# Packed attention and a mixture of experts on one core: batch 0 is routed in two groups of chunks, with batch 1's small products at their ends

## The chip, the cores and the metric

The kernel runs on 1 core of one Trainium2 chip. The metric is device time in microseconds (us) of one execution. The kernel before takes 422.11 us, the median of three runs (421.89 to 422.68). A core has five engines with an instruction queue each: PE (TensorE, matrix products), DVE (VectorE), ACT (ScalarE), POOL (GpSimd) and SP (SyncE, which here only issues transfers). Each runs its queue strictly in order and waits on semaphores for the others.

## The reference, cut to what matters

```python
def sm_attn(qq, kk, vv):                       # for 8 batches x 8 heads, S = 576, D = 64
    s = scale * np.matmul(qq, kk.transpose(0, 1, 3, 2))
    s = s - np.max(s, axis=-1, keepdims=True)
    a = np.exp(s)
    a = a / (np.sum(a, axis=-1, keepdims=True) + 1e-09)
    return np.matmul(a, vv)
p_packed = sm_attn(p, k, v)                    # 32 packed rows a head
attn = sm_attn(q, p_packed, p_packed)          # 576 rows a head
x = attn.transpose(0, 2, 1, 3).reshape(B * S, H * D)       # 4608 x 512

xn, en = x / norm(x), expert_emb / norm(expert_emb)
logits = xn @ en.T / tau                       # 8 experts
expert_idx = np.argmax(logits, axis=1)
gate_w = softmax(logits)[arange(N), expert_idx]
for e in range(8):
    mask = expert_idx == e
    h = np.maximum(x[mask] @ w1[e], 0.0)       # 512 -> 1024
    out[mask] = gate_w[mask, None] * (h @ w2[e])           # 1024 -> 512
```

## The kernel before, in words

The eight batches of 576 rows are worked one after the other. Each batch guesses one expert for all its rows, loads that expert's w1 and w2, and computes the feed-forward network (FFN) with them; rows whose expert turns out to be another one would be done again at the end (none are here). Products are made of 32-bit values split in a high and a low part, in three passes (`PASSES`).

The order of the work is written out by hand: `ffn` of batch b is a generator, and at each of its `yield`s the main loop advances the attention of batch b+1 (`step_att`) and the gates of batch b. For batch 0 the table `PLAN` says, letter by letter, what stands at each yield: `a` a step of batch 1's attention, `d` a transposition of batch 1's queries, `r` a step of batch 0's `route`, `w` one split of a w2 tile, `g` a step of batch 0's gates. Every engine then gets its instructions in the order in which this Python code records them.

The pieces that the change touches, for batches 0 and 1:

- `route` (L752 to L841) makes the attention rows in 5 chunks of 128 (the last of 64) with `product` (L766 on PE), squares them on ACT (L778) and sums the logits on DVE (L781), then finds each row's expert. Each chunk lies in a PSUM tile `pt` of the pool `pb`, which has 2 buffers. Before, batch 0 goes chunk by chunk; all later batches go in two groups, chunks 0 and 1, then chunks 2, 3 and both halves of 4.
- `pack_slowly` (L577) ends batch 1's packed attention: `pair_turn` (L501 on PE), its copy to `T` (L598), `row_logits` (L512 on PE), `logits_out` (L521). Then come `guess` (L619; its product L629, its DVE work L635 to L640, and a register load by SP), the load of w1 (L891), `att2` with `query_scores` (L270 on PE) and the softmax of the second attention, and the load of w2 (L899).
- The softmax works on two halves of the columns, 0 and 1: `unpack` (L675, DVE), `biggest` (L680, DVE), `shift` (L686), `expo` (L689, ACT), `total` (L695 to L697, DVE), `norm` (L701), `turn` (L704, DVE), `high` (L710, ACT), `low` (L715). The string `ENG1` gives for batch 1 the engine of shift 0, shift 1, norm 0, norm 1, low 0 and low 1: `v` is DVE, `p` is POOL.
- `counts` (L846 on PE) counts rows by expert; `gates` (L859 to L881) makes the gate of each row on DVE, with one exponential on ACT (L872); `gates_main` (L1394) adds the sum of the hits.
- In `ffn`, the product L1039 takes the 64 last rows through w2 into a tile `pf`; L1057 takes the four chunks c = 0 to 3 of the others through w2, 24 matmuls each. The tiles `pf` come from the pool `ps`, which has 3 buffers. The L1039 tile is stored (L1406, ACT, scaled by the gate) in the middle of chunk 1; its buffer is the one that chunk 2 of L1057 takes.

```python
    ps = ctx.enter_context(tc.tile_pool(name="ps", bufs=3, space=bass.MemoryType.PSUM))
    ...
                    if f == STF and len(last) > late:
                        store(*last.pop(0))
```

Of the kernel before, what the change touches and what calls it, by code (L numbers as in the profile page):

```python
# [9 lines left out]
F32 = mybir.dt.float32  # L10
# [7 lines left out]
P = 128  # L18
# [9 lines left out]
def kernel(  # L28
# [499 lines left out]
    def att1(x, nat, queries=None, other=None):  # L528

        def pack(queries, other):  # L530
# [46 lines left out]
        def pack_slowly():  # L577
# [16 lines left out]
            yield  # L594
# [10 lines left out]
        if x.halves:  # L605
            for g in range(NG):
                key_max(x, g)
                yield
                key_exp(x, g)
                yield  # L610
            yield from pack_slowly()
        else:
            asked = queries or all_queries(x, nat)
            yield from pack(asked, other)
            if queries is None:
                drain(asked)
# [33 lines left out]
    def att2(x, after=None, first=False, b1=False, eng1="vvvvvv"):  # L650
# [69 lines left out]
        if not first:  # L720
            query_scores(x)
            yield from idle(3 if x is bat[1] else 2)
# [34 lines left out]
    def route(x):  # L757
# [36 lines left out]
        if x is bat[0]:  # L794
            for c in range(NC5):
                pt = units()
                for g in range(NG):
                    product(c, g, pt[:, :, g])
                yield
                sums(c, pt[:, :, :NG], lg[:, c], ss[:, c : c + 1])  # L800
        else:
            lg4 = sm.tile([P, E], F32, name="lg4", tag="lg4", bufs=1)
            ss4 = sm.tile([P, 1], F32, name="ss4", tag="ss4", bufs=1)
            for cs in ((0, 1), (2, 3)):
                pts = [units() for _ in cs]
                for c, pt in zip(cs, pts):
                    for g in range(NG):
                        product(c, g, pt[:, :, g])
                if cs[0]:
                    for g, pt in enumerate(pts):  # L810
                        product(4, g, pt[:, :, NG])
                yield
                for c, pt in zip(cs, pts):
                    sums(c, pt[:, :, :NG], lg[:, c], ss[:, c : c + 1])
                    yield
            sums(4, pts[0][:, :, NG:], lg[:, 4], ss[:, 4:5])
            sums(4, pts[1][:, :, NG:], lg4, ss4)
            yield
            nc.vector.tensor_tensor(out=lg[64:, 4], in0=lg[64:, 4], in1=lg4[64:], op=ALU.add)
            nc.vector.tensor_tensor(out=ss[64:, 4:5], in0=ss[64:, 4:5], in1=ss4[64:], op=ALU.add)  # L820
# [298 lines left out]
    def att_main(b):  # L1119
        x = bat[b]  # L1120
        if b:
# [3 lines left out]
            yield from att1(x, nat_main(b), queries, bat[b - 1] if b > 1 else None)  # L1125
            sync = b == 1
            queue = nc.sync if sync else nc.gpsimd
# [9 lines left out]
        if b:  # L1137
            if b > 1:
                yield
            for _ in range(3 if b == 1 else 2):  # L1140
                yield next(second)
            load_w2(x, x.e, queue)
            if b == 1:
                yield from idle(3)
# [249 lines left out]
    def gates_main(b):  # L1394
        x = bat[b]
        yield from gates(x)
        hit = sm.tile([1, E], F32, name="hit", tag="hit", bufs=1)
# [3 lines left out]
    def store_main(b):  # L1401
# [33 lines left out]
    ENG1 = "vvppvp"  # L1435
# [5 lines left out]
        "aqwd", "aawrr", "awd", "rdwra", "rwa", "rwa", "", "a", "aag", "aag",  # L1441
# [8 lines left out]
    def route_first():  # L1450
        yield from route(bat[0])
        yield from idle(2)
        counts(bat[0])
# [164 lines left out]
```

## Time and profile before

| what | value |
|---|---|
| three runs | 421.89, 422.11, 422.68 us |
| profiled execution | 420.91 us, span 419.2 us from its first to its last instruction |
| mean granted clock of TensorE | 0.995 |
| PE busy | 408.4 us (97% of the span), 4036 matmul records |
| DVE, ACT, POOL busy | 307.2, 202.5, 158.7 us |

The span is what the trace shows; the time of the execution is 1.7 us longer. The profiled execution lies 1.2 us below the median of the three runs, so a difference read from the trace is put onto the median as it is. All start times below are us from the start of the span. In a timeline, instructions of one kind that follow each other are merged into one row: its start, its length to the end of the last one, the count, and in brackets how long the engine was idle before it and what ended that. The records of PE are its passes: a 32-bit matmul has two records, an L1057 matmul one.

### The profile page before, as it was taken

How to read it: one execution, taken by the hardware profiler on the slowest of the kernel's cores; microseconds unless marked ns; L12 is line 12 of the kernel's file. 1: busy time of each engine (PE TensorE's matmuls, PEld its weight loads, DVE VectorE, ACT ScalarE, POOL GpSimd, SP SyncE). 2: the span in 40 equal slices, each digit the busy share in tenths (PEclk: the TensorE clock that was granted, in tenths of full speed). 3: DMA queues.
4: the chain of work that ended last, by engine and by line, in shares of the span. 5: the costliest groups of instructions: out<-in, count | busy, mean ns of one | idle time of the engine just before them, and what ended most of it. 6: DMA issues, size and time to landing. Idle time of an engine off the chain costs nothing.

```text
span 419.2 us, 11033 instructions
## 1 busy us (share of the span) xinstructions
PE 408.4 (97%) x4036; PEld 327.9 (78%) x4037; DVE 307.2 (73%) x941; ACT 202.5 (48%) x473; POOL 158.7 (38%) x197
## 2 busy tenths in 40 slices
PE   7899999999999999999999999999999999999993
PEld 4758677697878978698777978789786987779783
DVE  3677696588977889769886889778897798566500
ACT  4577705762365714754146622656146631576110
POOL 2345714437204561336414381136613273142200
PEclk9999999999999999999999999999999999999998
DMA  8999896977999479886999669886899819310012
GB/s 225 331 338 236 220 296 221 229 189 187 298 298 235 116 216 294 284 201 172 267 316 228 169 172 280 301 216 177 225 317 262 195 39 344 121 48 5 20 48 54
DMA packets 42607, 87.93 MB, mean 210 GB/s; under 512 B 11690, under 2 KB 20906, under 8 KB 42546
## 3 DMA queue, kind: packets, MB, share of 16 engines
q1 hardware_dynamic: 35280, 61.44, 54.2%
q0 software_dynamic: 6720, 25.17, 18.4%
q8 instruction: 34, 0.56, 0.6%
q10 hardware_dynamic: 546, 0.54, 0.6%
q14 instruction: 27, 0.22, 0.2%
HBM read 77.68 MB, written 9.44 MB: 208 GB/s over the span
## 4 chain that ended last, share of the span: by engine, by line
PE 91%; DMA 4%; ACT 1%; DVE 1%; POOL 1%; SPq 0%; issue 0%; ACTq 0%; POOLq 0%
PE pf L1057 43%; PE pf L1004 24%; PE pf L1039 7%; PE pt L766 5%; DMA nat<-in_k 4%; PE pt L934 3%; PE pt L396 2%; PE pt L270 2%; PE pt L331 2%; PE pt L1233 1%; PE pu L501 0%; DMA out<-o 0%; PE pt L477 0%; PE pu L512 0%; ACT st L689 0%; PE pt L464 0%
## 5 line engine op out<-in xcount | busy, mean ns | idle before, releaser
L1057 PE MATMUL pf<-w2s,hT 128*128 128x512 f32 (+1 forms) x792 | 183.9, 388 | 0.0
L1057 PEld LDWEIGHTS pf<-w2s,hT 128*128 128x128 f32 x792 | 143.1, 188 | 39.3 <-issue 9.4
L910 POOL TENSOR_TENSOR w2s<-w2r,w2s 128x512 fp32r<-128x512 f32 x64 | 81.2, 1285 | 86.1 <-ACT w2s L909 85.3
L1004 PE MATMUL pf<-AT,G 128*128 128x288 f32 x720 | 102.1, 298 | 0.4 <-DVE hT L1009 0.2
L1004 PEld LDWEIGHTS pf<-AT,G 128*128 128x128 f32 x720 | 97.2, 188 | 4.3 <-issue 1.5
L1009 DVE SCALAR_TENSOR_TENSOR hT<-pf,hT 128x224 fp32r<-128x224 f32 (+1 forms) x128 | 52.2, 413 | 30.3 <-ACT hT L1008 29.9
L1008 ACT ACTIVATE hT<-pf 128x224 fp32r<-128x224 f32 (+1 forms) x128 | 49.3, 386 | 42.8 <-PE pf L1004 40.1
L1406 ACT ACTIVATE o<-pf,gate 128x512 f32<-128x512 f32 (+1 forms) x41 | 26.0, 635 | 32.2 <-PE pf L1057 21.2
L909 ACT CAST w2s<-w2r 128x512 fp32r<-128x512 f32 x64 | 38.7, 618 | 0.2
L291 DVE STREAM_TRANSPOSE kt<-nat 128x576 f32<-128x576 f32 x52 | 38.1, 759 | 0.0
L778 ACT ACTIVATE scr<-pt 128x512 f32<-128x512 f32 (+2 forms) x47 | 25.0, 532 | 18.0 <-PE pt L766 17.0
L1039 PE MATMUL pf<-w2r,h 128*64 128x256 f32 x256 | 33.3, 388 | 0.0
L715 POOL TENSOR_TENSOR AT<-at,AT 128x576 fp32r<-128x576 f32 x7 | 9.9, 1411 | 49.1 <-ACT AT L710 49.1
L383 POOL TENSOR_TENSOR qs<-p 128x320 f32<-128x320 f32 x12 | 10.6, 881 | 45.4 <-ACT p L364 45.4
L689 ACT ACTIVATE st<-st 128x576 f32<-128x576 f32 (+1 forms) x17 | 11.1, 657 | 33.8 <-DVE st L686 32.6
L872 ACT ACTIVATE lg<-lg 128x40 f32<-128x40 f32 x8 | 1.9, 237 | 48.4 <-DVE lg L868 48.4
L781 DVE TENSOR_REDUCE lg<-pt 128x8 f32<-128x32 f32 (+2 forms) x47 | 8.7, 185 | 22.0 <-ACT scr L778 21.7
L766 PEld LDWEIGHTS pt<-ppx,at 64*128 64x128 f32 x320 | 19.7, 186 | 6.2 <-issue 3.6
L1039 PEld LDWEIGHTS pf<-w2r,h 128*64 128x64 f32 x256 | 19.4, 137 | 4.9 <-PE pu L501 1.0
L766 PE MATMUL pt<-ppx,at 64*128 64x136 f32 x320 | 23.1, 287 | 0.0
L710 ACT CAST AT<-at 128x576 fp32r<-128x576 f32 x15 | 10.1, 675 | 22.6 <-DVE at L704 22.5
L364 ACT ACTIVATE p<-pt,qnm 128x160 f32<-128x160 f32 x48 | 17.8, 398 | 0.0
(213 smaller groups left out, 474.9 us busy)
## 6 DMA issues: line engine op xcount, KB each, us to landing
nat<-in_q SPq DMA_DIRECT2D x112, 140.0 KB, 3.5
nat<-in_k SPq DMA_DIRECT2D x96, 140.0 KB, 4.0
w1t<-in_moe_w POOLq DMA_DIRECT2D x12, 1024.0 KB, 9.3
w2r<-in_moe_w POOLq DMA_DIRECT2D x24, 512.0 KB, 16.0
out<-o SPq DMA_DIRECT2D x124, 64.0 KB, 2.1
w2r<-in_moe_w SPq DMA_DIRECT2D x8, 512.0 KB, 10.3
vn<-in_v SPq DMA_DIRECT2D x24, 160.0 KB, 3.8
vn<-in_v SPq DMA_DIRECT2D x48, 80.0 KB, 3.9
```

The lines of the kernel that those rows point to most:

```text
L291: nc.vector.transpose(kt.rearrange("p (c i) -> p c i", i=32), t)
L364: nc.scalar.activation(x.p1[g][:, n * QW : n * QW + QW], area(x, g)[:, n // 2, n % 2], AF.Exp, bias=x.nm[:, at : at + 1],)
L766: nc.tensor.matmul(to[:, half], x.at[at, g, n : n + P], x.ppx[at, g], start=True, stop=True, tile_position=(64 * half, 0),)
L778: nc.scalar.activation(scr[r, :, : pt.shape[2]], pt[r, :, :, : 2 * D], AF.Square, accum_out=sss[r])
L909: nc.scalar.copy(t[:, 0], raw)
L910: nc.gpsimd.tensor_tensor(out=t[:, 1], in0=raw, in1=t[:, 0].bitcast(F32), op=ALU.subtract)
L1004: nc.tensor.matmul(pf[:, :HS], w, r, start=(n == 0), stop=(n == len(ops) - 1))
L1008: nc.scalar.activation(hT[:, 0, f, cs], pf[:, :n], AF.Relu)
L1009: nc.vector.scalar_tensor_tensor(out=hT[:, 1, f, cs], in0=pf[:, :n], scalar=0.0, in1=hT[:, 0, f, cs].bitcast(F32), op0=ALU.max, op1=ALU.su ...
L1039: nc.tensor.matmul(pf[64 * hf : 64 * hf + 64, :256], h4[:, f], x.w2r[f // 2][:, f % 2, hf * 256 : hf * 256 + 256], start=(f == 0), stop=(f ...
L1057: nc.tensor.matmul(pf[:, :w], hT[:, a, f, c * P : (c + 1) * P], x.w2s[f][:, m, at : at + w], start=(f == 0 and i == 0), stop=(f == NF - 1 ...
L1406: nc.scalar.activation(o[:, :w], pf[:, :w], AF.Copy, scale=x.gate[:, c : c + 1])
```

## The change

Batch 0's `route` now uses the code of the other batches with the groups in the other order: chunks 0, 1 and both halves of 4 in the first group, 2 and 3 in the second. The table `PLAN` puts batch 1's `pair_turn` at the end of the first group and its `row_logits` at the end of the second, and takes several steps of batch 0's FFN between; `query_scores` of batch 1 is recorded before its `guess`, and both stand within the first chunk of L1057. `counts` of batch 0 goes with that of batch 1 into batch 2's attention, and its sum of hits (`hits(0)`) too. Shift 0 of batch 1 goes from DVE to POOL (`ENG1`). The steps of batch 0's gates stand at other places between those of batch 1's softmax.

```diff
             quarter_totals(x, sums)
-            if other:
-                counts(other, pt[:1, 256 : 256 + NC5 * E])
+            for n, other in enumerate(others):
+                counts(other, pt[:1, 256 + n * NC5 * E : 256 + (n + 1) * NC5 * E])
             next(queries)
             yield
-            if other:
+            for other in others:
                 counted(other)
+                if other is bat[0]:
+                    hits(0)
...
-        if not first:
+        if not first and not x.s2:
             query_scores(x)
-            yield from idle(3 if x is bat[1] else 2)
+            yield from idle(2)
...
-        if x is bat[0]:
-            for c in range(NC5):
-                pt = units()
+        lg4 = sm.tile([P, E], F32, name="lg4", tag="lg4", bufs=1)
+        ss4 = sm.tile([P, 1], F32, name="ss4", tag="ss4", bufs=1)
+        for cs in ((0, 1), (2, 3)):
+            pts = [units() for _ in cs]
+            rest = bool(cs[0]) != (x is bat[0])
+            for c, pt in zip(cs, pts):
                 for g in range(NG):
                     product(c, g, pt[:, :, g])
+            if rest:
+                for g, pt in enumerate(pts):
+                    product(4, g, pt[:, :, NG])
+            yield
+            for c, pt in zip(cs, pts):
+                sums(c, pt[:, :, :NG], lg[:, c], ss[:, c : c + 1])
+                if c != 3 or rest:
+                    yield
+            if rest:
+                sums(4, pts[0][:, :, NG:], lg[:, 4], ss[:, 4:5])
+                sums(4, pts[1][:, :, NG:], lg4, ss4)
                 yield
-                sums(c, pt[:, :, :NG], lg[:, c], ss[:, c : c + 1])
...
             sync = b == 1
+            if sync:
+                query_scores(x)
...
-    ENG1 = "vvppvp"
+    ENG1 = "pvppvp"
...
-        "aqwd", "aawrr", "awd", "rdwra", "rwa", "rwa", "", "a", "aag", "aag",
-        "aagr", "agr", "gar", "ga", "gra", "g", "ga", "", "", "a",
+        "awd", "aw", "radw", "ra", "rd", "rw", "w", "w", "ra", "r",
+        "r", "ar", "a", "a", "aa", "ga", "ga", "gga", "gg", "gga",
...
     def route_first():
         yield from route(bat[0])
-        yield from idle(2)
-        counts(bat[0])
```

What this does to three queues is read from the built programs. The first place is PE, from the first L1039 product of batch 0 to its w2 product L1057, whose line is L1053 after the change (L1039 becomes L1035, L766 becomes L767, L629 becomes L630). `ppx,at` are the products of `route`, `ident,ppx` is the pair turn, `enT,T` the row logits, `ppx,itaus` the guess, `kt,T` the query scores, `oh,ones` the counts. Before, the last twelve blocks up to the long one:

```order
L1039 MATMUL pf<-w2r,h_519 64x256 x2
L766 MATMUL pt<-ppx,at 128x136 x8
L1039 MATMUL pf<-w2r,h_519 64x256 x2
L766 MATMUL pt<-ppx,at 128x136 x4
L512 MATMUL pu<-enT,T 64x8 x4
L1039 MATMUL pf<-w2r,h_519 64x256 x2
L629 MATMUL pu<-ppx,itaus 64x8 x2
L1039 MATMUL pf<-w2r,h_519 64x256 x4
L270 MATMUL pt<-kt,T 32x288 x16
L1039 MATMUL pf<-w2r,h_519 64x256 x2
L1057 MATMUL pf<-w2s,hT 128x512 x9
L846 MATMUL pu<-oh,ones 1x40
```

Ahead of these stand four more (L1039 x2, L766 x8, L1039 x2, L501 x2). After the change the whole stretch is:

```order
L1035 MATMUL pf<-w2r,h_519 64x256 x4
L767 MATMUL pt<-ppx,at 128x136 x12
L501 MATMUL pu<-ident,ppx 128x128 x2
L1035 MATMUL pf<-w2r,h_519 64x256 x12
L767 MATMUL pt<-ppx,at 128x136 x8
L512 MATMUL pu<-enT,T 64x8 x4
L1053 MATMUL pf<-w2s,hT 128x512 x9
L270 MATMUL pt<-kt,T 32x288 x16
L630 MATMUL pu<-ppx,itaus 64x8 x2
L1053 MATMUL pf<-w2s,hT 128x512 x45
```

Sixteen short blocks have become nine; the products are the same, but for the counts, which now stand in batch 2. In both programs the 45 matmuls of the last block end with the first six of chunk 2.

The second place is DVE, where batch 1's softmax (`st`, `mx2`, `s2`) and batch 0's gates (`rq_t`, `gy`, `lg`, `gate`) are mixed, up to shift 1 (`st_1024` before, `st_1016` after). Before, the last twelve of them:

```order
L875 TENSOR_REDUCE gate_1021<-lg_837 128x5
L876 TENSOR_SCALAR gate_1021<-gate_1021 128x5
L675 STREAM_TRANSPOSE st_1024<-pt_947 128x288 x2
L878 RECIPROCAL gate_1021<-gate_1021 128x5
L880 COPY gate_1021<-gate_1021 64x1
L1398 TENSOR_TENSOR hit_1032<-cnt_1008,sel_358 1x8
L1399 TENSOR_REDUCE rest_f_118<-hit_1032 1x1
L680 TENSOR_REDUCE mx2_1035<-st_1024 128x18
L695 TENSOR_REDUCE s2_1043<-st_991 128x18
L696 TENSOR_SCALAR s2_1043<-s2_1043 128x18
L697 RECIPROCAL s2_1043<-s2_1043 128x18
L686 TENSOR_TENSOR st_1024<-st_1024,mx2_1035 128x576
```

After:

```order
L861 TENSOR_SCALAR gy_1009<-gy_1009 128x5
L696 TENSOR_REDUCE s2_1038<-st_996 128x18
L697 TENSOR_SCALAR s2_1038<-s2_1038 128x18
L698 RECIPROCAL s2_1038<-s2_1038 128x18
L863 RECIPROCAL gy_1009<-gy_1009 128x5
L864 TENSOR_TENSOR lg_838<-lg_838,gy_1009 128x40
L871 TENSOR_REDUCE gate_1048<-lg_838 128x5
L872 TENSOR_SCALAR gate_1048<-gate_1048 128x5
L874 RECIPROCAL gate_1048<-gate_1048 128x5
L876 COPY gate_1048<-gate_1048 64x1
L687 TENSOR_TENSOR st_1016<-st_1016,mx2_1025 128x576
```

Shift 1 now stands directly behind the gate's last instruction and behind the sums of half 0. Shift 0 is no longer in this queue, and the first six gate instructions, which stood ahead of the first `unpack`, now stand behind the first `biggest`.

The third place is ACT, from the last squares of batch 0's `route` to the store of the L1039 tile (`o`). Before:

```order
L778 ACTIVATE scr_908,ss_838<-pt_892 64x512
L909 CAST w2s_920<-w2r_426 128x512
L872 ACTIVATE lg_837<-lg_837 128x40
L689 ACTIVATE st_991<-st_991 128x576
L689 ACTIVATE st_1024<-st_1024 128x576
L1406 ACTIVATE o_1059<-pf_828,gate_1021 128x256
```

After:

```order
L779 ACTIVATE scr_922,ss_839<-pt_902 128x512
L779 ACTIVATE scr_928,ss_839<-pt_903 128x512
L690 ACTIVATE st_996<-st_996 128x576
L868 ACTIVATE lg_838<-lg_838 128x40
L690 ACTIVATE st_1016<-st_1016 128x576
L1409 ACTIVATE o_1058<-pf_828,gate_1048 128x256
```

The gate's exponential has moved between the two of the softmax; the store `o` stands directly behind the exponential of half 1 (`st_1024` before, `st_1016` after) in both.

## Rows read from the trace of the kernel before

**Rows 1.** The page's first part: busy time, share of the span, instructions.

```profile
PE 408.4 (97%) x4036; PEld 327.9 (78%) x4037; DVE 307.2 (73%) x941; ACT 202.5 (48%) x473; POOL 158.7 (38%) x197
```

**Rows 2.** Stretches: length, each engine's busy time, PEclk, DMA; a middle batch.

```profile
130.20:178.90 48.70, 48.70 (x498) 39.68 (x497) 40.37 (x118) 23.80 (x56) 19.59 (x25) 1.00 0.81 227
```

**Rows 3.** Waits of PE: for whom, us in total, times, longest; the last.

```profile
PE pf L1004 <- DVE hT L1009: 0.2, 1, 0.2
```

**Rows 4.** Timeline of PE, batch 0's FFN: start, length, line, tiles, count.

```profile
44.49 0.65 PE L1039 MATMUL pf<-w2r,h 128*64 128x256 f32 x4
...
56.33 10.50 PE L1057 MATMUL pf<-w2s,hT 128*128 128x512 f32 x45
66.76 1.20 PE L766 MATMUL pt<-ppx,at 64*128 64x136 f32 x16
67.89 0.50 PE L1057 MATMUL pf<-w2s,hT 128*128 128x512 f32 x1
```

**Rows 5.** Timeline of DVE and ACT, batch 1's softmax and the store before chunk 2.

```profile
54.46 0.15 DVE L92 TENSOR_SCALAR rq_i<-ss 128x5 int32<-128x5 int32 x1
...
55.40 0.84 DVE L675 STREAM_TRANSPOSE st<-pt 128x288 f32<-128x288 f32 x2
...
62.57 0.70 DVE L686 TENSOR_TENSOR st<-st,mx 128x576 f32<-128x576 f32 x1
63.30 0.69 ACT L689 ACTIVATE st<-st 128x576 f32<-128x576 f32 x1 [3.43 <-DVE st L686]
64.02 0.47 ACT L1406 ACTIVATE o<-pf,gate 128x256 f32<-128x256 f32 x1
```

**Rows 6.** Timeline of PE, the short blocks of batch 1's FFN.

```profile
97.47 0.38 PE L501 MATMUL pu<-ident,ppx 128*128 128x128 f32 x2
97.78 1.08 PE L1039 MATMUL pf<-w2r,h 128*64 128x256 f32 x8
98.69 0.35 PE L512 MATMUL pu<-enT,T 128*64 128x8 f32 x8
98.89 1.06 PE L1039 MATMUL pf<-w2r,h 128*64 128x256 f32 x8
99.79 0.29 PE L629 MATMUL pu<-ppx,itaus 128*64 128x8 f32 x3
...
101.84 1.20 PE L270 MATMUL pt<-kt,T 64*32 64x288 f32 x32
```

**Rows 7.** Timeline of DVE, batch 2's guess, batch 1's gates, batch 2's softmax.

```profile
100.17 0.16 DVE L635 MAX8 m<-pu 1x8 f32<-1x8 f32 x1
...
100.99 0.78 DVE L291 STREAM_TRANSPOSE kt<-nat 128x576 f32<-128x576 f32 x1
101.69 0.13 DVE L92 TENSOR_SCALAR rq_i<-ss 128x5 int32<-128x5 int32 x1
...
106.03 0.82 DVE L675 STREAM_TRANSPOSE st<-pt 128x288 f32<-128x288 f32 x2
...
107.67 0.76 DVE L686 TENSOR_TENSOR st<-st,mx 128x576 f32<-128x576 f32 x1
...
111.06 0.69 DVE L686 TENSOR_TENSOR st<-st,mx 128x576 f32<-128x576 f32 x1
```

**Rows 8.** Timeline of POOL and DVE where both work at once in batch 2.

```profile
114.03 1.41 POOL L715 TENSOR_TENSOR AT<-at,AT 128x576 fp32r<-128x576 f32 x1 [7.39 <-ACT AT L710]
...
114.41 1.65 DVE L701 TENSOR_TENSOR st<-st,s 128x576 f32<-128x576 f32 x1
```

**Rows 9.** Timeline of POOL, a shift of the whole width (batch 0).

```profile
25.07 1.16 POOL L686 TENSOR_TENSOR st<-st,mx 128x576 f32<-128x576 f32 x1 [0.29 <-PE pt L1233]
```

**Rows 10.** The page's groups: line, engine, tiles, count | busy, mean ns | idle.

```profile
L910 POOL TENSOR_TENSOR w2s<-w2r,w2s 128x512 fp32r<-128x512 f32 x64 | 81.2, 1285 | 86.1 <-ACT w2s L909 85.3
```

**Rows 11.** Stretches at the end of the span, columns as in Rows 2.

```profile
412.00:414.00 2.00, 0.81 (x7) 0.61 (x6) 0.00 (x0) 0.47 (x1) 0.00 (x0) 1.00 0.18 43
416.00:418.00 2.00, 0.00 (x0) 0.00 (x0) 0.00 (x0) 0.00 (x0) 0.00 (x0) 0.50 0.03 8
```

More of the change, by code (lines that the diff above doesn't have):

```diff
@@ L526, in all_queries, with att1, pack @@
             yield
-    def att1(x, nat, queries=None, other=None):
-        def pack(queries, other):
+    def att1(x, nat, queries=None, others=()):
+        def pack(queries, others):
             pack_tiles(x)
@@ L593, in pack_slowly @@
             pu = pc.tile([P, 512], F32, name="pu", tag="pu")
-            yield
             for g in range(NG):
@@ L613, in att1 @@
             asked = queries or all_queries(x, nat)
-            yield from pack(asked, other)
+            yield from pack(asked, others)
             if queries is None:
@@ L792, in units @@
             )
-        if x is bat[0]:
-            for c in range(NC5):
-                pt = units()
+        lg4 = sm.tile([P, E], F32, name="lg4", tag="lg4", bufs=1)
[4 more added lines that the diff above has]
+            for c, pt in zip(cs, pts):
                 for g in range(NG):
                     product(c, g, pt[:, :, g])
-                yield
-                sums(c, pt[:, :, :NG], lg[:, c], ss[:, c : c + 1])
[L801 to L820, printed above, removed]
+            if rest:
[9 more added lines that the diff above has]
+                sums(4, pts[1][:, :, NG:], lg4, ss4)
+                yield
+        nc.vector.tensor_tensor(out=lg[64:, 4], in0=lg[64:, 4], in1=lg4[64:], op=ALU.add)
+        nc.vector.tensor_tensor(out=ss[64:, 4:5], in0=ss[64:, 4:5], in1=ss4[64:], op=ALU.add)
         nc.vector.tensor_scalar_mul(lg, lg, itau)
@@ L1124, in att_main @@
             queries = all_queries(x, nat_main(b)) if b > 1 else None
-            yield from att1(x, nat_main(b), queries, bat[b - 1] if b > 1 else None)
+            yield from att1(x, nat_main(b), queries, bat[b - 1 if b > 2 else 0 : b] if b > 1 else ())
             sync = b == 1
+            if sync:
+                query_scores(x)
             queue = nc.sync if sync else nc.gpsimd
@@ L1139, in att_main @@
                 yield
-            for _ in range(3 if b == 1 else 2):
-                yield next(second)
+                for _ in range(2):
+                    yield next(second)
             load_w2(x, x.e, queue)
             if b == 1:
-                yield from idle(3)
+                yield
         yield from second
@@ L1396, in gates_main, with hits @@
         yield from gates(x)
+        if b:
+            hits(b)
+    def hits(b):
+        x = bat[b]
         hit = sm.tile([1, E], F32, name="hit", tag="hit", bufs=1)
```

## The prediction

> **What bounds the kernel now.** Read the page's busy times first: PE is busy for 97% of the span, the next engine (DVE) for 73% [rows 1]. An average can hide a stage, so the second view is the busy time by stretches: in a middle batch PE is busy for 48.70 of 48.70 us, while DVE has 8 us to spare and ACT and POOL more than half [rows 2]. Third, the list of PE's waits: it has six entries, and the latest in time is the 0.2 us of [rows 3], in batch 0's first FFN product; from there to the last matmul PE waits for nothing. So after the start the time is the sum of what stands in PE's queue. A shorter queue is worth its length, and a new wait costs its length less what the shorter queue gained before it. The other engines matter only where PE waits for them, so the fourth view is the timeline around the change, read for how close PE already comes to such a wait. One place is close: chunk 2 of L1057 takes the buffer of the L1039 tile, which ACT's store frees. The last block of 45 matmuls starts at 56.33 and the next block at 66.76 [rows 4], 0.232 us each; chunk 2 is its last six, so it starts 39 matmuls in, at 56.33 + 39 x 0.232 = 65.37. The store ends at 64.02 + 0.47 = 64.49 [rows 5]. The margin before is 0.9 us.
>
> **What PE's queue loses.** The products are the same, in nine blocks for sixteen, and the counts go (into batch 2, where four such products already stand side by side). Priced from the rows of blocks that run long: L1039 97.78 to 98.69, 0.91 for four; L501 97.47 to 97.78, 0.31; L512 98.69 to 98.89, 0.20 [rows 6]; eight products of `route` 66.76 to 67.89, 1.13 [rows 4], so 1.70 for twelve. From 44.49 [rows 4] the new queue runs: L1039 x4 to 45.40, `route` x12 to 47.10, pair turn to 47.41, L1039 x12 (2.73) to 50.14, `route` x8 to 51.27, row logits to 51.47, L1057 x9 (2.09) to 53.56, query scores (1.20 less their overlap with the next block, about 1.13 [rows 6]) to 54.69, guess (as the row logits, 0.20) to 54.89. The block of 45 would start there instead of at 56.33: 1.44 us earlier. I take 1.4, since a change of block costs a little on top of the nine matmuls. No wait should stand in this stretch: the second group of `route` needs PSUM tiles that ACT's four squares and DVE's sums must free, and the pair turn and twelve L1039 products lie between, 3.0 us of cover; if that cover is short it is by tenths, and it only eats into the 1.4 us.
>
> **What becomes of the store.** Chunk 2 would now start at 65.37 - 1.4 = 64.0. The store must by then have ended, and it stands on ACT directly behind the exponential of half 1, which waits for shift 1 on DVE. Shift 1 starts at 62.57, the store ends at 64.49 [rows 5]: 1.92 us from one to the other, all of it in a chain (0.70, 0.69, 0.47 and the hand-overs), and nothing in it changes. What changes is when shift 1 starts. I name two times: U, the start of batch 1's first `unpack`, and S, the start of shift 1.
>
> U before is 55.40 [rows 5]. In the changed queue `unpack` stands behind the guess, and the guess's product starts only at 54.69. From that product (99.79 [rows 6]) to the first maximum is 0.38 us, and from there to the next large instruction 0.82 [rows 7]: U = 55.9 at the earliest. At the latest it is 56.5: the last three splits of w2 now follow the four squares on ACT and run on POOL one behind the other, 3 x 1.285 = 3.9 us [rows 10] from about 50 on, and DVE's addition of the two halves of chunk 4 can fall into the third of them and wait for its end (below). I take 56.2.
>
> From U to S it is 62.57 - 55.40 = 7.17 us before [rows 5]. Into this stretch come six gate instructions that stood ahead of it (54.46 to 55.40, 0.94 [rows 5]); out of it go shift 0 (0.76 [rows 7]) and three small counting instructions, which I leave in: 7.35, the lower end. The upper end comes from batch 2, where nothing is interleaved: all of the gates, 101.69 to 106.03, and the softmax from `unpack` to shift 1, 106.03 to 111.06, less shift 0: 4.34 + 5.03 - 0.76 = 8.6 [rows 7]. I take 7.8, nearer to the row of this very batch.
>
> To this comes what shift 0 does on POOL. It takes 1.16 us there [rows 9], against 0.76 on DVE; the exponential behind it still comes in time for the sums of half 0. But it runs beside DVE's gate instructions. Where both engines had a two-operand instruction in SBUF, DVE's took 1.65 us instead of 0.76: it started at 114.41 and ended at 116.06, 0.62 us behind the end of POOL's at 115.44 [rows 8, 7], so it did its work only when POOL's was over. Shift 0 starts as soon as `biggest` is through, which is when DVE comes to the third gate instruction (`rq_t`, two operands in SBUF): a dead heat. If POOL is first, `rq_t`, the second `unpack` and all behind them stand for 1.1 us. Norm 0 is on POOL before and after, but then DVE was past it; now it meets the gate's last products, 0.4 to 1.0 us. Lower end of both: nothing; upper end 2.1. I take 1.1 + 0.4 = 1.5.
>
> [...]
>
> So S = 56.2 + 7.8 + 1.5 = 65.5, the store ends at 67.4, and PE, ready for chunk 2 at 64.0, waits 3.4 us. Against the 65.37 of before chunk 2 starts 2.0 us later. **The 1.4 us saved ahead of the wait are swallowed by it**; only the end of the store counts.
>
> **What comes behind.** The rest of PE's queue is as before, so the 2.0 us go to the end. Batch 1's `turn`s, its `route` and the w1 rows follow shift 1 on DVE and ACT in the same order as before, and PE comes to them later in relation to S than before (chunk 2 starts 1.9 us behind S, before 2.8, but norm 0 is ahead by more than that), so I see no second wait. The guess is two us later, and with it the loads of w1 and w2 for batch 1; PE wants them as much later. The two counts side by side in batch 2 cost a few hundredths. If one of these covers fails it adds a few tenths.
>
> **Sum.** 420.91 for the profiled execution, + 2.0 = 422.9; on the median of the runs, 422.11 + 2.0 = **424.1 us**. Ends of the terms: U 55.9, 7.35 and no block give a store at 65.2, -0.2 us; U 56.5, 8.6 and 2.1 give 69.1, +3.7 us.
>
> **The rivals.**
>
> 1. *The shorter queue pays and the store is in time.* Nine blocks for sixteen is worth 1.4 us: 420.7. For it: PE is the bound in every stretch [rows 1, 2]. Against it: the margin of the store was 0.9 us, less than what PE gains, and its chain starts later, not earlier. It decides from S below 62.1. With `unpack` not before 55.9 that needs 6.2 us from U to S, a full us under the 7.17 of before with more instructions in between. It could be so only if chunk 2's buffer is another than I take it for. Chance 0.07.
>
> 2. *The store is late, but POOL blocks nobody.* If DVE wins both dead heats, S = 55.9 to 56.2 + 7.35 to 7.8 and the store ends at 65.2 to 65.9: -0.2 to +0.6 us, 422.0 to 422.7, in the middle 422.3. For it: `rq_t` and shift 0 start within hundredths of each other. Chance 0.18.
>
> 3. *TensorE's clock falls in the wait.* At the end of the span the last matmuls run to 412.8 with a granted clock of 1.00 (2.4 GHz); with PE then idle it is 0.50 (1.2 GHz) from 416 on [rows 11]. Before the change nothing in the FFN leaves PE idle. In the new wait PE would be idle for 3 to 4 us, so the clock may fall in it, and the matmuls behind run at half rate until it rises again. No row here shows a rise: the price is nothing at the least, and if the low level lasts as long as the wait, 3.4 us at half rate, 1.7 us; twice that, 3.4 us. I take 1.9: 426.0. Chance 0.18. [...]
>
> The forecast itself (a wait of 2.5 to 4.5 us, clock held) has 0.57, with its own range 423.2 to 425.5.
>
> **How the numbers follow.** What a measurement of this kernel can tell from no change is 0.2%, 0.84 us: 421.27 to 422.95. Rival 1 is faster (0.07). Rival 2 is the same, nearly all of it (0.15), the rest slower. The forecast and rival 3 are slower, but for the forecast's lowest edge. Faster 0.07, same 0.17, slower 0.76. The range leaves out rival 1 and the top of rival 3: 422.0 to 426.4.
>
> **What would show it.** In the profile of the changed kernel the list of PE's waits should have a new first entry: L1053 for ACT, once, at about 64 us and 2.5 to 4.5 us long, ended by the store `o`. The block ahead of it should start at about 55. On DVE the first `unpack` should start at 55.9 to 56.5 and shift 1 at 64 to 66, with one `rq_t` of over 1 us if POOL blocks, and a small gate instruction near the end stretched in the same way. From the wait on every PE block should stand later than before by the same amount. The prediction is wrong if PE starts chunk 2 without waiting, if PE has a second wait of its own behind it (for a PSUM tile of `route` or for w1), or if the matmuls behind the wait take twice their 0.232 us, which is rival 3.

## The result and the profile after

The changed kernel took 425.24 us (median of 11 runs, 423.02 to 427.67), the kernel before 421.93 us (median of 11 runs in the same comparison): a ratio of 1.0089, interval 1.0067 to 1.0112. By the ratio it is slower by 3.8 us, by the two medians by 3.3, where 2.0 were predicted. The profiled execution took 425.99 us with a span of 424.3 us.

All the times in the rows below are of the profiled execution named, from the start of its span.

The page's first part of the changed kernel answers to [rows 1]:

```profile
PE 409.2 (96%) x4036; PEld 329.2 (78%) x4037; DVE 308.9 (73%) x943; ACT 202.6 (48%) x475; POOL 159.7 (38%) x198
```

The work is the same to within 1 or 2 us on every engine, 0.8 on PE, and the span is 5.1 us longer. So 4.3 of the 5.1 us are time in which PE stands. The list of PE's waits says where (for whom, us in total, times, longest; its first entry and two others):

```profile
PE pf L1053 <- ACT o L1409: 2.6, 1, 2.6
PE pf L1199 <- DMA nat<-in_k: 2.3, 2, 1.2
...
PE pu L512 <- DVE T L570: 0.2, 1, 0.2
```

The first is the wait that was forecast. The second is of the start, and differs from one execution to the next (0.8 in the profile before). The third was not forecast. PE's timeline in batch 0's FFN answers to [rows 4]:

```profile
45.37 1.08 PE L1035 MATMUL pf<-w2r,h 128*64 128x256 f32 x8
...
52.21 0.41 PE L512 MATMUL pu<-enT,T 128*64 128x8 f32 x8
52.54 2.34 PE L1053 MATMUL pf<-w2s,hT 128*128 128x512 f32 x9
54.81 1.20 PE L270 MATMUL pt<-kt,T 64*32 64x288 f32 x32
55.95 0.40 PE L630 MATMUL pu<-ppx,itaus 128*64 128x8 f32 x4
56.27 9.15 PE L1053 MATMUL pf<-w2s,hT 128*128 128x512 f32 x39
67.99 2.13 PE L1053 MATMUL pf<-w2s,hT 128*128 128x512 f32 x6 [2.56 <-ACT o L1409]
70.05 2.19 PE L767 MATMUL pt<-ppx,at 64*128 64x136 f32 x16
72.17 3.12 PE L1053 MATMUL pf<-w2s,hT 128*128 128x512 f32 x12
```

The queue starts 0.88 us later than before (45.37 for 44.49); the keys of batch 0 came later. From there the block of 45 is reached in 56.27 - 45.37 = 10.90 us, before in 11.84: 0.94 us gained. It breaks after 39 matmuls, and the six of chunk 2 stand apart behind a gap of 2.56 us. These six and the products behind them are slow: 70.05 - 67.99 = 2.06 us for the six (39 matmuls of the same kind take 0.232 each, six 1.39), and 72.17 - 70.05 = 2.12 for the sixteen records of `route`, 1.13 in [rows 4]. The stretches tell why (columns as in [rows 2]; the eighth group, before the DMA share, is the granted clock):

```profile
68.00:69.00 1.00, 1.00 (x4) 0.85 (x5) 0.93 (x4) 0.50 (x1) 0.00 (x0) 1.00 1.04 385
69.00:70.00 1.00, 1.00 (x3) 0.33 (x1) 0.48 (x1) 0.00 (x0) 0.98 (x1) 0.50 1.04 381
...
71.00:72.00 1.00, 1.00 (x12) 0.92 (x10) 0.73 (x3) 0.66 (x2) 0.00 (x0) 0.50 0.09 19
72.00:73.00 1.00, 1.00 (x7) 0.75 (x4) 0.19 (x1) 0.97 (x4) 0.91 (x1) 0.80 0.02 8
```

PE was idle from 65.4 to 68.0, worked for a microsecond at a granted clock of 1.00, and went on at 0.50 for 3.41 us (68.99 to 72.40). Two passes of L1053, 512 columns wide, start 0.227 us apart at 1.00 (64.58 and 64.81) and 0.426 us apart at 0.50 (69.07 and 69.49): 2.26 and 1.20 columns a ns. The trace gives the clock as a share of full speed; no run shows a frequency, as rival 3 and e4 name it, and no sum uses one. The chain that PE waited for answers to [rows 5] (timelines of DVE, POOL and ACT):

```profile
57.16 0.83 DVE L676 STREAM_TRANSPOSE st<-pt 128x288 f32<-128x288 f32 x2
...
58.96 1.08 DVE L103 TENSOR_TENSOR rq_t<-rq_h,rq_i 128x5 f32<-128x5 f32 x1
...
65.16 0.52 DVE L872 TENSOR_SCALAR gate<-gate 128x5 f32<-128x5 f32 x1
...
66.10 0.76 DVE L687 TENSOR_TENSOR st<-st,mx 128x576 f32<-128x576 f32 x1
...
58.86 1.16 POOL L687 TENSOR_TENSOR st<-st,mx 128x576 f32<-128x576 f32 x1 [2.26 <-DVE mx L681]
64.49 1.16 POOL L702 TENSOR_TENSOR st<-st,s 128x576 f32<-128x576 f32 x1 [4.47 <-DVE gy L863]
...
66.89 0.68 ACT L690 ACTIVATE st<-st 128x576 f32<-128x576 f32 x1 [1.99 <-DVE st L687]
67.48 0.46 ACT L1409 ACTIVATE o<-pf,gate 128x256 f32<-128x256 f32 x1
```

U is 57.16, S 66.10, the store ends at 67.94. `rq_t` of five columns took 1.08 us because shift 0 had begun on POOL 0.10 us ahead of it, and both ended at 60.0; the gate instruction at 65.16 ran beside norm 0, took 0.52 us and ended within 0.03 us of it (65.68, 65.65); in e6, where POOL is idle beside it, it takes 0.17 (at 67.69).

The wait that nobody forecast is in batch 2 (first DVE's row of the copy `T` in the kernel before, then timelines of DVE and PE in the changed kernel):

```profile
98.15 0.41 DVE L568 COPY T<-pu 128x256 f32<-128x256 f32 x1
```

```profile
99.48 0.19 DVE L849 TENSOR_REDUCE cnt<-pt 1x8 f32<-1x40 f32 x1
99.70 0.48 DVE L1401 TENSOR_TENSOR hit<-cnt,sel 1x8 f32<-1x8 f32 x1
100.22 0.15 DVE L1402 TENSOR_REDUCE rest_f<-hit 1x1 f32<-1x8 f32 x1
...
103.07 0.41 DVE L570 COPY T<-pu 128x256 f32<-128x256 f32 x1
...
102.20 1.08 PE L1035 MATMUL pf<-w2r,h 128*64 128x256 f32 x8
103.53 0.41 PE L512 MATMUL pu<-enT,T 128*64 128x8 f32 x8 [0.25 <-DVE T L570]
```

Batch 0's count and its hits now stand on DVE ahead of batch 2's pairs. The copy `T` starts 0.87 us behind PE's eight L1035 records (103.07 - 102.20), before 0.37 (98.15 - 97.78), and PE, which in [rows 6] goes from the eight L1039 records to the row logits in 0.91 us, needs 103.53 - 102.20 = 1.33.

### The profile page after: what moved, and what is told of

It reads as the page before. It is cut to its first block, busy times and chain, and to the rows that moved or that the text cites. A ratio compares the mean times of both kernels' runs of the same rounds, so it can differ in the third digit from the quotient of the medians.

```text
span 424.3 us, 11038 instructions
## 1 busy us (share of the span) xinstructions
PE 409.2 (96%) x4036; PEld 329.2 (78%) x4037; DVE 308.9 (73%) x943; ACT 202.6 (48%) x475; POOL 159.7 (38%) x198
## 4 chain that ended last, share of the span: by engine, by line
PE 87%; DVE 5%; ACT 3%; DMA 2%; issue 1%; POOL 1%; SPq 0%; DVEq 0%; ACTq 0%; POOLq 0%
PE pf L1053 40%; PE pf L1000 23%; PE pf L1035 6%; PE pt L767 5%; PE pt L930 3%; PE pt L396 2%; PE pt L331 2%; DMA nat<-in_k 2%; PE pt L270 2%; PE pf L1199 1%; PE pt L1231 1%; ACT scr L779 1%; PE pt L464 1%; ACT st L690 0%; DVE hT L1005 0%
## 5 line engine op out<-in xcount | busy, mean ns | idle before, releaser
L1053 PE MATMUL pf<-w2s,hT 128*128 128x512 f32 (+1 forms) x792 | 184.9, 389 | 2.6 <-ACT o L1409 2.6
L1053 PEld LDWEIGHTS pf<-w2s,hT 128*128 128x128 f32 x792 | 143.3, 188 | 42.1 <-issue 9.3
L779 ACT ACTIVATE scr<-pt 128x512 f32<-128x512 f32 (+1 forms) x48 | 25.2, 525 | 20.2 <-PE pt L767 19.2
L1035 PE MATMUL pf<-w2r,h 128*64 128x256 f32 x256 | 32.2, 386 | 0.0
L782 DVE TENSOR_REDUCE lg<-pt 128x8 f32<-128x32 f32 (+1 forms) x48 | 8.8, 186 | 22.7 <-ACT scr L779 22.7
L767 PEld LDWEIGHTS pt<-ppx,at 64*128 64x128 f32 x320 | 20.5, 194 | 6.0 <-issue 3.9
L767 PE MATMUL pt<-ppx,at 64*128 64x136 f32 x320 | 23.9, 295 | 0.0
L1035 PEld LDWEIGHTS pf<-w2r,h 128*64 128x64 f32 x256 | 19.7, 137 | 5.0 <-PE pu L501 1.0
```

The costliest lines, as they stand in the source:

```text
L767: nc.tensor.matmul(to[:, half], x.at[at, g, n : n + P], x.ppx[at, g], start=True, stop=True, tile_position=(64 * half, 0),)
L779: nc.scalar.activation(scr[r, :, : pt.shape[2]], pt[r, :, :, : 2 * D], AF.Square, accum_out=sss[r])
L1035: nc.tensor.matmul(pf[64 * hf : 64 * hf + 64, :256], h4[:, f], x.w2r[f // 2][:, f % 2, hf * 256 : hf * 256 + 256], start=(f == 0), stop=(f ...
L1053: nc.tensor.matmul(pf[:, :w], hT[:, a, f, c * P : (c + 1) * P], x.w2s[f][:, m, at : at + w], start=(f == 0 and i == 0), stop=(f == NF - 1 ...
```

## Experiments

The theory: the loss is the wait for the store, the clock behind it, and the counts in batch 2. The rivals: POOL's blocking of DVE is the main loss; the clock is an accident of one execution, or not the clock but the loads of w1 and w2 slow PE there; something in the queue itself.

Two distances are read from every trace. A runs from the first short w2 product (44.49 before) to the first row of six `pf<-AT,G` of the next batch (81.50 before), 37.01 us; B from there to the same row a batch later, 48.68 us. What A and B gain or lose, divided by the time before, is the ratio that the trace explains; the ratio measured stands beside it. The rows of the kernel before, then of the changed kernel:

```profile
81.50 0.95 PE L1004 MATMUL pf<-AT,G 128*128 128x288 f32 x6
...
130.18 0.95 PE L1004 MATMUL pf<-AT,G 128*128 128x288 f32 x6
```

```profile
85.84 0.95 PE L1000 MATMUL pf<-AT,G 128*128 128x288 f32 x6
...
135.07 0.95 PE L1000 MATMUL pf<-AT,G 128*128 128x288 f32 x6
```

| kernel | A | B | A and B against before | by the trace | measured [interval] |
|---|---|---|---|---|---|
| changed kernel | 40.47 | 49.23 | +4.01 | 1.0095 | 1.0089 [1.0067, 1.0112] |
| e9, it again | 38.89 | 49.27 | +2.47 | 1.0059 | 1.0088 [1.0073, 1.0103] |
| e1, store first | 38.46 | 49.25 | +2.02 | 1.0048 | 1.0044 [1.0026, 1.0063] |
| e2, early copy | 38.42 | 49.27 | +2.00 | 1.0047 | 1.0044 [1.0025, 1.0062] |
| e3, shift 0 on DVE | 38.82 | 49.23 | +2.36 | 1.0056 | 1.0083 [1.0056, 1.0111] |
| e4, filler | 38.92 | 49.26 | +2.49 | 1.0059 | 1.0054 [1.0036, 1.0072] |
| e10, filler again | 38.94 | 49.27 | +2.52 | 1.0060 | 1.0076 [1.0056, 1.0095] |
| e5, hits late | 38.92 | 48.90 | +2.13 | 1.0051 | 1.0067 [1.0054, 1.0081] |
| e6, four edits | 37.09 | 48.93 | +0.33 | 1.0008 | 1.0016 [1.0006, 1.0026] |
| e7, before with shift 0 on POOL | 37.44 | 48.69 | +0.44 | 1.0010 | 1.0013 [1.0000, 1.0025] |
| e8, five edits | 36.21 | 48.94 | -0.54 | 0.9987 | 0.9989 [0.9977, 1.0001] |

**e1: shift 1, and with it the exponential of half 1, recorded one step later, so that ACT does the store first.**

```diff
-        "r", "ar", "a", "a", "aa", "ga", "ga", "gga", "gg", "gga",
-        "a", "a", "a", "a", "ga", "a", "aa", "aa", "aa", "a",
+        "r", "ar", "a", "a", "aa", "ga", "ga", "gga", "gg", "gg",
+        "aa", "a", "a", "a", "ga", "a", "aa", "aa", "aa", "a",
```

> One step of batch 1's softmax is recorded one slot later, so that on ACT the store of the L1039 tile stands ahead of the exponential of half 1; nothing else moves. Theory (the end of the store sets chunk 2, and it is late because it stands behind shift 1 and the exponential): the store starts when the gate is through, 0.1 us before shift 1 starts, instead of 1.4 us behind it; PE's wait for it falls from 2.6 us to 1.2 us, the clock falls less often or not at all, and the time is 1.3 us (no fall in either) to 3.0 us below the changed kernel: a ratio to the kernel before of 1.002 to 1.006. Rival (the wait only moves to the next thing that is late, turn 0 of batch 1): PE waits as long as before at batch 1's route products, ratio 1.009 as the changed kernel.

**e2: ACT copies the L1035 tile out of PSUM early; the store scales the copy.**

```diff
+                    if late and c == 0 and f == 4:
+                        held = sb.tile([P, DM], F32, name="o", tag="o", bufs=3)
+                        nc.scalar.copy(held[:, :256], last[0][1][:, :256])
+                        last[0] = (4, held, 0, 256)
```

> ACT copies the L1039 tile out of PSUM in chunk 0 (0.5 us of ACT, which idles there) and the store scales the copy; so chunk 2's buffer is free long before it is wanted. Theory: no wait for the store at all, chunk 2 starts directly behind chunk 1; the next late thing is turn 0 of batch 1, some 0.8 us behind PE. Ratio to the kernel before 1.000 to 1.003 (-0.9 us from the shorter queue, +0.8 at turn 0, +0.5 in batch 2, no fall of the clock). Rival (the softmax of batch 1 is as late as the store): the wait moves whole to the route products, 2 us or more, ratio 1.006 to 1.009.

PE's waits of e1, then of e2:

```profile
PE pf L1053 <- ACT o L1409: 1.2, 1, 1.2
...
PE pt L767 <- DVE lg L782: 0.5, 1, 0.5
```

```profile
PE pt L767 <- DVE lg L782: 1.0, 1, 1.0
PE pt L767 <- DVE at L705: 0.9, 1, 0.9
```

Both take the store out of PE's way, and both give back part of it: e1 keeps 1.2 us of it and gets 0.5 at batch 1's `route`; in e2 nothing waits for `o`, and turn 0 (`at`) and the sum `lg` cost 1.9 us in its place. With the wait gone PE arrives earlier at everything that hangs on shift 1. The clock stayed at 1.00 from 64 to 74 us in both traces, and the medians lie 2.1 and 2.0 us over the kernel before: the store's wait was the first of a row, each hidden by the one ahead of it. e1 came out as expected. e2's ratio of 1.0044 lies between its two expectations: turn 0 was forecast (0.8 us, 0.91 measured), the 1.03 us for `lg` behind it was not.

**e3: shift 0 of batch 1 on DVE as before.**

```diff
-    ENG1 = "pvppvp"
+    ENG1 = "vvppvp"
```

> Only the engine of shift 0 of batch 1 goes back to DVE. Theory (POOL's shift 0 blocks DVE's two-operand gate instruction for 1 us): the first rq_t takes 0.17 us instead of 1.08, DVE gets 0.7 us of shift in its place, shift 1 starts 0.2 to 0.4 us earlier, PE's wait is 2.2 to 2.4 us instead of 2.6; ratio 1.007 to 1.009, hardly to be told from the changed kernel by time, but plain in the trace. Rival (POOL takes work off DVE for nothing): shift 1 starts 0.7 us later and the wait is 3.3 us, ratio 1.010 or more.

DVE's timeline of e3:

```profile
59.69 0.17 DVE L103 TENSOR_TENSOR rq_t<-rq_h,rq_i 128x5 f32<-128x5 f32 x1
...
65.91 0.76 DVE L687 TENSOR_TENSOR st<-st,mx 128x576 f32<-128x576 f32 x1
```

The stop of `rq_t` is gone (0.17 for 1.08), but DVE now does shift 0 itself (0.76), and from U (57.09) to S it is 8.82 us instead of 8.94. PE waited 2.47 us, where 2.2 to 2.4 were expected. Where shift 0 runs is worth a tenth of a microsecond here: the rival of POOL falls. That does not make the stop free: `rq_t` loses 0.91 us by it, but shift 0 takes 0.76 us on DVE instead. The stop by norm 0 is there in e3 too, and no run takes it away alone.

**e7: the kernel before, with shift 0 of batch 1 on POOL** (the opposite edit, in the other kernel).

```diff
-    ENG1 = "vvppvp"
+    ENG1 = "pvppvp"
```

> The kernel before with shift 0 of batch 1 moved from DVE to POOL, as in the changed kernel, and nothing else. The longer shift on POOL (1.16 us for 0.75) and DVE's stops beside it (1.08 us for 0.17 in the changed kernel's trace) stand ahead of the pair turns. Theory (POOL's part of the loss is real but is lost only where something stands behind it without slack): turn 0 at PE has slack in the kernel before, 0.3 us or more are left of it, and the time is the same, ratio 0.999 to 1.001. Rival (POOL's blocking of DVE was the main loss): turn 0 is waited for by 0.5 to 1.1 us and the ratio is 1.001 to 1.003.

DVE's timeline of e7:

```profile
57.20 1.16 DVE L108 SCALAR_TENSOR_TENSOR gy<-rq_t,gy 128x5 f32<-128x5 f32 x1
...
64.84 0.78 DVE L704 STREAM_TRANSPOSE at<-st 128x576 f32<-128x576 f32 x1 [1.05 <-POOL st L701]
```

POOL's shift started at 57.17 and stopped an instruction of 0.17 us for a whole one again. Turn 0 waits for norm 0 as long as in the kernel before (1.05 us for 1.04), but starts 64.84 - 44.23 = 20.61 us behind the first short w2 product, before 64.31 - 44.49 = 19.82. PE lost 0.14 us ahead of `route`'s first block and 0.25 us in its second. A grew by 0.43 us and the ratio is 1.0013. That is about a seventh of what the change costs, so the stop is not the main loss, but it is more than the 0.001 that I allowed and lies at the rival's lower edge: the kernel before had less slack at turn 0 and behind it than I read from it.

**e4 and e10: ten w2 matmuls, whose result is thrown away, in PE's queue where it waits.**

```diff
+                if late and c == 2:
+                    pu = pc.tile([P, 512], F32, name="pu", tag="pu")
+                    for _ in range(FILL):
+                        nc.tensor.matmul(
+                            pu, hT[:, 0, 0, :P], x.w2s[0][:, 0], start=True, stop=True
+                        )
...
+    FILL = 10
```

> Ten matmuls of the L1057 kind (0.23 us each) on a bank that nobody uses then stand ahead of chunk 2, so that PE works through its wait; their result is thrown away. Theory (the matmuls behind the wait run at half the clock because PE stood idle): the clock stays at 1.00 (2.4 GHz) between 68 and 73 us, the route products of batch 1 take 1.1 us instead of 2.1, and the executions lie 0 to 1.7 us lower than those of the changed kernel, closer together: ratio 1.005 to 1.007. Rival (something else slows PE there, such as the w1 and w2 loads that fill the DMA engines): the route products still take 2.1 us, ratio 1.009.

> The kernel of e4_fill unaltered: ten L1057-type matmuls, whose result is thrown away, stand in PE's queue where PE waits for the store, so PE is busy there and does no more useful work. Both theories: ratio to the kernel before 1.0045 to 1.0065, as before. By the theory that the lower clock raises the changed kernel's median, this is 0.0025 or more under the changed kernel on the same chip; by the rival it is equal within 0.001.

**e9: the changed kernel again**, beside e10 on one chip.

> The changed kernel unaltered, on the same chip as a second run of e4_fill, since the two were timed on different chips so far (ratios to the kernel before 1.0089 [1.0067, 1.0112] and 1.0054 [1.0036, 1.0072]). What the traces account for without a lower clock: -0.94 in the queue, +2.56 wait, +0.1 at its edge, +0.55 in batch 2, together +2.3 us, ratio 1.0054. Theory (the clock falls behind the wait often enough to raise the median by 1 us or more): ratio 1.0080 to 1.0095, and 0.0025 or more above e4 on this chip. Rival (the fall is an exception of the profiled execution, the rest was the chip or the start): ratio 1.0045 to 1.0065, equal to e4 within 0.001.

PE's timeline of e9, with a stretch of its trace (columns as above), and PE's timeline of e4:

```profile
66.89 1.66 PE L1053 MATMUL pf<-w2s,hT 128*128 128x512 f32 x6 [2.56 <-ACT o L1409]
68.49 1.20 PE L767 MATMUL pt<-ppx,at 64*128 64x136 f32 x16
69.61 3.00 PE L1053 MATMUL pf<-w2s,hT 128*128 128x512 f32 x12
...
83.17 0.95 PE L1000 MATMUL pf<-AT,G 128*128 128x288 f32 x6
```

```profile
68.00:69.00 1.00, 1.00 (x11) 0.63 (x11) 0.39 (x1) 0.00 (x0) 1.00 (x1) 1.00 1.05 375
```

```profile
63.91 2.43 PE L1053 MATMUL pu<-w2s,hT 128*128 128x512 f32 x10
66.64 1.66 PE L1059 MATMUL pf<-w2s,hT 128*128 128x512 f32 x6 [0.30 <-ACT o L1416]
```

In e9 PE waits the same 2.56 us, and behind it the six matmuls take 1.60 and the sixteen records 1.12: the clock did not fall. The DMA share is 1.05 there, as high as in the first trace (1.04), so the loads of w1 and w2 are not what slowed PE. From the wait's end to the end of A it is 83.17 - 66.89 = 16.28 us, in the first trace 85.84 - 67.99 = 17.85; so the fall cost 1.57 us where it came. How often it comes the mean clock of an execution tells: it was 0.992 in the traced execution with a fall, 0.995 in e9's without. Of the 17 runs of the changed kernel in both comparisons 6 have 0.992 or less (median 425.4 us), 11 have 0.994 or more (median 424.4). With the filler all 16 have 0.994 or more. The kernel before has 0.992 in 2 of the 77 executions timed beside these variants, so a low mean is not always this fall; and three of the changed kernel's eleven with a high mean took 426.3 to 426.7 us, so the time varies for other reasons too. The fall looks neither like the rule nor like an accident: about one execution in three, if the mean clock tells it rightly, and none seen where PE was kept busy. For the median neither prediction was met: e9's ratio is in the theory's range, but side by side the filler is 0.0012 faster, where 0.0025 or equality within 0.001 was asked, and the intervals overlap. The filler's own ratio was 1.0054 on one chip and 1.0076 on another, over the 1.0065 that both theories allowed; the two intervals overlap, so 0.2% cannot be told here.

**e5: in batch 2 the older count and both hits pieces stand behind the copy `T`.**

```diff
-            for other in others:
+            for other in others[-1:]:
                 counted(other)
-                if other is bat[0]:
-                    hits(0)
...
+            for other in others[:-1]:
+                counted(other)
+                hits(0)
...
```

> The changed kernel; in the later batches the second count and the two hits pieces of the batch before stand on DVE behind the copy T instead of ahead of the pair scan. In the trace of the changed kernel L1401 x2, L849 x2 and L1402 stand there from 99.48 to 100.50 us, the copy T ends late, the pair logits (L512) wait 0.25 us for it, and batch 2's distance between L1004-type rows is 49.23 us against 48.68. Theory (this order on DVE costs about 0.55 us, once): no wait of L512 for T is left, the distance is back at 48.7, and the time is 0.4 to 0.6 us under the changed kernel's, ratio to the kernel before about 0.0012 lower (1.0077 for 1.0089). Rival (what the counts cost is the two short PE blocks themselves, or the chip run's spread): the wait goes and the distance stays at 49.1 or more. The wait for o in batch 1 (2.6 us) and the clock behind it are not touched and stay.

The wait of L512 for `T` left the list, and B fell from 49.23 to 48.90. So 0.33 of the 0.55 us were DVE's order ahead of `T`. Of the 0.22 left, 0.13 stand between the second eight short w2 records and the query scores (3.08 us from one to the other, before 2.95): the hits now end on DVE at 101.64, the copy of the row logits behind them at 101.72, and the guess that needs it starts at 101.77. The rest is in hundredths. Neither prediction was met: the distance lies between them.

**e6: four edits together**: the early copy with its store a chunk later, e5's order, both shifts and norms of batch 1 on DVE, and the last gate steps behind turn 0.

```diff
...
-    ENG1 = "pvppvp"
+    ENG1 = "vvvvvp"
...
-        "r", "ar", "a", "a", "aa", "ga", "ga", "gga", "gg", "gga",
-        "a", "a", "a", "a", "ga", "a", "aa", "aa", "aa", "a",
+        "r", "ar", "a", "a", "aa", "ga", "ga", "ga", "", "a",
+        "ga", "a", "a", "a", "ga", "ga", "aga", "aga", "aa", "a",
```

> Four edits to the changed kernel together: ACT copies the first columns of the PSUM tile of L1039 out at the fifth block, so that chunk 2 no longer stands on the store; the store itself is recorded a chunk later; shift 0, shift 1 and both norms but the last run on DVE, and the gates' later parts stand behind shift 1 and turn 0; counts and hits in batch 2 behind T. Theory (the loss is made of the wait for o with the lower clock behind it, of turn 0 and the logits that come late once that wait is gone, and of the counts in batch 2): no wait of PE over 0.3 us between the first block and the w2 product, distance from the first block of batch 1 to L1000 x6 under 37.5 us (37.01 before, 38.4 with the early copy alone), time 0.5 to 1.0 us under the kernel before (ratio 0.9976 to 0.9988), as the queue saving of 0.94 us is then alone. Rival (DVE becomes the bound of this stretch: it now carries 3 shifts and norms of 0.75 us each more): turn 0 or the logits are waited for by 0.5 to 1.5 us, ratio 1.000 to 1.003.

The timeline of ACT, DVE and PE in e6:

```profile
68.57 0.67 ACT L713 CAST AT<-at 128x576 fp32r<-128x576 f32 x1 [1.36 <-DVE at L707]
69.15 0.59 ACT L781 ACTIVATE scr<-pt 128x512 f32<-128x512 f32 x1
...
69.86 0.19 DVE L784 TENSOR_REDUCE lg<-pt 128x8 f32<-128x32 f32 x1 [0.46 <-ACT scr L781]
...
70.11 1.92 PE L769 MATMUL pt<-ppx,at 64*128 64x136 f32 x24 [0.63 <-DVE lg L784]
```

Chunk 2 and turn 0 no longer hold PE and A is under 37.5 us (37.09), as the theory has it, but the gain is not there: PE's second block of `route` waits 0.63 us for PSUM, and the ratio is 1.0016. The first block was done at 66.4; its squares stand on ACT behind the copy `high` of half 1, which waits 1.36 us for turn 1 on DVE. So a wait of the rival's size came; whether DVE's load or ACT's order makes it, e8 decides.

**e8: as e6, and batch 1's first `route` group is recorded ahead of norm 1 and turn 1.**

```diff
+        r = route(x) if b else None
+        if b == 1:
+            for n, _ in enumerate(second):
+                yield
+                if n in (10, 11):
+                    for _ in range(n - 9):
+                        next(r)
+                        yield
         yield from second
...
-            steps = {"r": route(x), "f": flips}
+            steps = {"r": r, "f": flips}
...
-            for turn in TURNS:
+            for turn in TURNS[3 * (b == 1) :]:
...
-        "ga", "a", "a", "a", "ga", "ga", "aga", "aga", "aa", "a",
+        "ga", "a", "a", "a", "g", "", "aagaa", "agga", "aa", "a",
```

> As the four edits together (e6_best), and also the first four products of batch 1's pair scores, their squares on ACT and their sums on DVE stand ahead of norm 1, turn 1 and the copy hi 1, not behind them. In the trace of e6_best PE waits 0.63 us for the sum lg (L784) at 69.86 us, which stands on ACT behind the copy hi 1 (68.57 us), though its products were done at 66.43; the wait and the slow restart of the block (1.92 us for 1.66) are all that is left of the loss in batch 1. Theory (PE is now held only by this order): no wait over 0.2 us between the first block and the w2 product, the distance from the first block of batch 1 to the first L1004-type row of batch 2 is 36.2 us (37.09 in e6_best, 37.01 before), and the time is 0.3 us under to 0.1 us over the kernel before, ratio 0.9993 to 1.0002. Rival (DVE carries too much in this stretch, so the order only moves the wait to turn 1 or to the copies): a wait of 0.3 to 0.8 us at the second block of products, ratio 1.0005 to 1.0015.

PE's timeline of e8:

```profile
56.31 10.51 PE L1055 MATMUL pf<-w2s,hT 128*128 128x512 f32 x45
66.75 1.20 PE L769 MATMUL pt<-ppx,at 64*128 64x136 f32 x16
...
71.00 1.66 PE L769 MATMUL pt<-ppx,at 64*128 64x136 f32 x24
```

No wait is left in the stretch, the block of 45 runs through, and A is 36.21, where 36.2 was expected: of the queue's 0.94 us 0.80 are there at last. So the order made e6's wait (squares and sums behind norm 1, turn 1 and the copy), not DVE's load, which is the same here, and the queue itself is not at fault. The 0.26 that B has lost come off. 420.69 us for 421.19, ratio 0.9989 [0.9977, 1.0001]: a gain of 0.5 us by the median, a little more than expected, whose interval just reaches no change.

## Why the prediction was right, and where it was not

Taking the 0.88 us of the later start out of the times of the changed kernel's trace:

| step | predicted | measured |
|---|---|---|
| what the queue loses | 1.4 | 0.94 |
| U | 56.2 | 56.28 |
| U to S, with POOL | 7.8 + 1.5 = 9.3 | 8.94 |
| S | 65.5 | 65.22 |
| end of the store | 67.4 | 67.06 |
| PE ready for chunk 2 | 64.0 | 64.55 |
| the wait | 3.4 | 2.56 |
| chunk 2 later than before | 2.0 | 1.74 |
| batch 2 | hundredths | 0.55 |
| clock behind the wait | 1.9 at 0.18 | 1.57, in about a third of the runs |

**The mechanism was right.** The shorter queue ends in a new wait for the store, once, at the place and from the chain that were named, and only the end of the store counts. Both meetings with POOL went as taken: `rq_t` stood for 0.91 us more than its 0.17, the gate instruction for 0.35. Without them U to S is 8.94 - 1.26 = 7.68 us, for the 7.8 taken. The addition of the two halves of chunk 4 stood too, for 1.15 us from 53.76 to the end of POOL's third split at 54.9, as U's upper end had allowed. In the first meeting POOL was ahead: `rq_t` began 0.10 us after its shift and ended with it. Where DVE was ahead, as rival 2 supposes, the kernel before has a case in which DVE lost nothing: batch 1's shift 1 began at 62.57, 0.23 us ahead of POOL's norm 0, and took 0.70 us, as short as any of the fourteen shifts on DVE, while the norm (62.80) took 1.48 us for the 1.16 of the one at 29.05.

**The queue was mis-sized**, by 0.46 us. The blocks were priced from [rows 6], where short products stand between L1039 products. Next to the wide L1053 products they cost more: the row logits 52.54 - 52.21 = 0.33 for 0.20, the guess 0.32 for 0.20, the nine L1053 matmuls 2.27 for 2.09 (9 x 0.232). The same nine already took 2.26 us in their old place, in the kernel before:

```profile
53.91 2.33 PE L1057 MATMUL pf<-w2s,hT 128*128 128x512 f32 x9
56.17 0.23 PE L846 MATMUL pu<-oh,ones 128*1 128x40 f32 x2
```

**The store was put 0.34 us too late** by the upper guess for U to S. Both errors shorten the wait (2.56 for 3.4), but only the second enters the delay of chunk 2 (1.74 for 2.0), since what the queue gains is swallowed whatever its size.

**Two terms were missing from the forecast.** The counts in batch 2 were priced by what they are on PE, hundredths; they stand on DVE ahead of a copy that PE waits for, and cost 0.55 us with everything around them. And the clock: rival 3 had its price about right and its chance too low, and the fall did not come in the wait, as it has it, but a microsecond behind its end. The changed kernel's first trace is rival 3, by the sign that the prediction named (six matmuls in 2.06 us for 1.39); e9's is the forecast with the clock held. PE's waits for turn 0 and the sum `lg`, which the prediction did not see, stayed hidden behind the store and came out in e1 and e2.

The profiled execution adds up: +0.88 start, -0.94 queue, +2.56 wait, +1.57 clock, +0.55 batch 2 make +4.6 of the +5.1 us; 0.15 more stand at the edges of the wait (16.28 in e9 against 16.13 before), the rest in hundredths elsewhere. Without a fall the trace explains +2.5 us (e9); with one execution in three 1.6 us longer, a mean of +3.0. Measured are +3.8 and +3.7 by the ratios of the two comparisons, +3.3 and +3.5 by their medians. The missing 0.3 to 0.8 us are in executions without a trace and stay open. The start could hold them (the first short w2 product begins between 43.94 and 45.41 us in the ten traces of the changed kernel and its variants, before at 44.49), but nothing shows that it is later in the changed kernel than before: the ten have a mean of 44.53.

The prediction lies 1.1 us under the median, within its range. By the medians the loss is 3.3 us for the 2.0 forecast: the delay of chunk 2 was 0.3 too high, the edges of the wait add 0.15, the two terms that it lacked weigh 0.55 and, on the mean, about 0.5, and the rest is the part left open. Nothing in the prediction stood for batch 2's 0.55 us; the range took it in because it was wide enough for rival 3 and the upper ends of U to S, and so far the hit is luck. Two ends are slips of its sums, and nothing hangs on them: a wait of 4.5 us less the 1.4 gained gives 425.2, not 425.5, and rival 2's -0.2 us gives 421.9, not 422.0.

## What to carry to other kernels

Before shortening the queue of the bounding engine, find the next place where it takes a buffer, and read when that is freed: the gain is lost there unless the freeing chain moves too. When a wait is taken away, walk on to the next one with the new arrival time; here there were three in a row (store, turn, sum of the scores), and only in the kernel that moved all three does the trace show the shorter queue's gain. Price a moved block from a row with the same neighbours, and a moved trifle by who stands behind it in every queue, not by its own length.

## What the runs showed of the hardware

In the changed kernel's first trace the clock fell after a wait of 2.56 us, not in it but 1.00 us after PE had resumed (67.99, 68.99), and stayed at 0.50 for 3.41 us while PE was busy. Behind waits of 2.47, 2.56 and 2.58 us in other traced executions (e3, e9, e5) it was 1.00, up to 74 us in e3 and e5 and from 68 to 72 us in e9. An instruction of 0.17 us, five columns wide, was stopped for 0.9 to 1.0 us by a POOL instruction that had begun 0.03 to 0.10 us earlier (58.96 in the changed kernel, 57.20 in e7).
